# Two S4D convolution layers with routed FFNs: shorter setups, four-tile first transform step in layer two, new order

## The chip, the cores and the metric

The kernel runs on one core of a Trainium2 chip. A core has five engines with queues of their own: TensorE (PE, matmuls; PEld in the profile is its weight load), VectorE (DVE), ScalarE (ACT), GpSimd (POOL) and SyncE (SP, which issues most DMAs). The metric is the device time of one launch in microseconds. All data are 32-bit floating point numbers.

## The reference

`x` has 2048 tokens of 512 numbers. Each of two layers does

```python
x = x + S4D(layernorm(x))          # convolution over the tokens, per channel
x = x + routed_ffn(layernorm(x))   # SwiGLU FFN on two tokens, all others pass
```

The convolution's taps are built from the parameters (128 states for each channel), and it is done with transforms of twice the length:

```python
dt = exp(log_dt);  A = -exp(log_A_real) + 1j * A_imag
C = (C_real + 1j * C_imag) * dt[:, None]
P = exp((A * dt[:, None])[:, :, None] * arange(2048))
K = 2 * einsum("dn,dnl->dl", C, P).real
y = irfft(rfft(u, 4096) * rfft(K, 4096))[:2048] + u * D_skip
```

The routed part scores each token (`r = x @ w_r`), takes the two with the highest score, sends them through `(silu(x @ w_gate) * (x @ w_up)) @ w_down`, scales by `sigmoid(r)` and adds the result back. Both layers have the same parameters, so K is built once.

## The kernel before

The 512 channels are four chunks of 128; tokens lie as 128 partitions of 16 each (`z [128,16,128]`).

**Setups** (`setup`, lines L553 to L650). From A, C and dt they make planes of decays and phases for every (state, channel) pair: modulus and angle of C with Abs, a reciprocal, Arctan, Sin and corrections by quadrant (L592 to L618), fractions of turns in 32-bit integers (L620 to L631), shifted copies (L634), exponentials of the decay (L647). `setup(0, 1, ...)` does it for the first chunk, 128 wide, and keeps its planes in SBUF; `setup(1, 4, ...)` does it for the other three, 384 wide, and writes its planes to DRAM. An ACT function that is in another table than the one before needs an ACT_TABLE_LOAD.

**Kernel taps** (`KStep`, 32 of them, eight for each chunk). Each builds 1024 columns: POOL adds phases (L675) and multiplies decays (L689, L694), ACT makes sines and magnitudes (L705, L699, L708), DVE multiplies them (L716 to L723), PE sums over the states on 32-column tiles (pk, L731) and transforms (kq, L751).

**Convolution of a chunk** (`Conv`). A transform in two steps: the first, `f1a`, multiplies z with a block-diagonal constant into zf (recorded at L414, in `halves`, which writes a result with two 64-column tiles, weights of 128 rows). Each of its eight waves is four matmuls of 256 columns into a PSUM tile of one bank, 128x512, from a pair of such buffers (tag "f1"). `f1b` (L855) transposes it on DVE into g. Then, in eight groups, pu (second step, PE, L774), the product p with the kernel's spectrum (DVE, L864), the sums y (POOL and DVE, L877 and L879), pv (inverse step, PE), its copy v (ACT, L1108), a trip of v through DRAM (vd), and po (L919), the last inverse step, added to x. The last chunk of a layer takes another way to po (`fin_0`, `fin_t`, `fin_mm` L901).

**Routed part** (`Routed`). The choice of the tokens (about L1325 to L1470), pg and pu (up projections, PE, L1476) and pd (down, L1496), and the way back. `keep_awake` issues pairs of matmuls without use ("aw") where PE would have nothing to do.

**What sets the order.** Every unit of this work goes into an agenda with a number from the table `PLAN` (for each lane, one number for its k-th unit). `run` sorts the agenda by number and calls the units, and `in_order` binds the instructions of every engine to the order in which they are issued:

```python
def put_in(lane, f, *a):
    k = counts[lane] = counts.get(lane, -1) + 1
    agenda.append((PLAN[lane][k], (lane, k), f, a))
```

So an instruction that waits holds up all those behind it on its engine.

Of the kernel before, what the change touches and what calls it, by code (L numbers as in the profile page):

```python
# [19 lines left out]
D = 512  # L20
# [22 lines left out]
    ],  # L43
    x0=[103, 57, 141, 123],
    stat0=[105, 107, 104, 110, 99, 58, 59, 97, 161, 150, 144, 142, 128, 131, 124, 125],
    phase8=[
        94, 108, 109, 112, 85, 179, 199, 240, 259, 220, 346, 354, 364, 375, 358, 456, 470, 476, 492, 478, 606, 630, 631, 633, 589,
        707, 731, 782, 783, 791, 907, 933, 934, 946, 896, 1055, 1078, 1081, 1082, 1057,
    ],
    decay8=[  # L50
        87, 117, 121, 126, 106, 207, 247, 266, 277, 214, 371, 389, 390, 391, 393, 466, 474, 505, 509, 511, 601, 602, 603, 638,
        627, 740, 774, 775, 777, 727, 901, 929, 950, 960, 895, 1095, 1096, 1100, 1108, 1137,
    ],
    phase_0=[
        114, 113, 166, 152, 260, 264, 304, 330, 376, 407, 406, 445, 493, 538, 577, 518, 647, 676, 702, 690, 784, 787, 865, 815,
        947, 970, 1020, 1033, 1140, 1180, 1224, 1085,
    ],
    phase=[
        115, 146, 167, 165, 265, 270, 317, 339, 377, 408, 442, 446, 498, 544, 581, 539, 648, 677, 704, 692, 793, 798, 874, 886,
# [1813 lines left out]
```

## Time and profile before

| what | us |
|---|---|
| runs | 527.70, 527.08, 525.61 (median 527.08) |
| profiled execution, own time | 528.49 |
| its span | 526.7 |
| PE busy | 420.1 (80%) |
| DVE busy | 419.7 (80%) |
| ACT busy | 386.0 (73%) |
| POOL busy | 317.0 (60%) |

The span runs from the first to the last instruction of the profile; 1.8 us of the execution's own time lie outside it. Shares are averages over stages: first loads and setups (to about 65 us), kernel taps beside layer one's convolution (to about 330), layer one's routed part (to 390, overlapped with layer two's first chunk), layer two's convolution (to 475), and its routed part with the output. In lists by line, "x64" is a count of instructions, then come busy us and mean ns, then idle time ahead of them with what ended it. In lists in order of time the first number is the start and the second the duration of the row. A float matmul is two records.

### The profile page before, as it was taken

What the parts mean: (1) busy time and instruction counts of PE and PEld (TensorE: products, weight loads), DVE (VectorE), ACT (ScalarE), POOL (GpSimd) and SP (SyncE); (2) the same over time, 40 slices, a digit from 0 to 9 for tenths busy, and PEclk for the clock granted to TensorE, in tenths of its full rate; (3) what the DMA queues carried; (4) which work ended last, traced back from release to release, by engine and by line L of the source; (5) the groups of instructions that cost most, each with busy time, mean ns of one, the idle gap of its engine ahead of it and who ended that gap; (6) DMA issues with size and microseconds to landing.
All of it is one profiled execution on the core that took longest, in us unless ns stands there. A gap on an engine that the chain in (4) does not pass through costs nothing.

```text
span 526.7 us, 17177 instructions
## 1 busy us (share of the span) xinstructions
PE 420.1 (80%) x6976; PEld 322.5 (61%) x6976; DVE 419.7 (80%) x987; ACT 386.0 (73%) x862; POOL 317.0 (60%) x334
## 2 busy tenths in 40 slices
PE   1014377999989998799999986999799999878468
PEld 1013256888758976579857843557568788654134
DVE  7999997877958998688998479766667799889851
ACT  5998999999969978859755345643656958548892
POOL 0496689997958567736702945234606889977300
PEclk9999999999989999899999999799999999999779
DMA  7243988879655885667593999564574748846634
GB/s 254 85 195 113 297 326 326 231 188 233 181 147 169 221 222 174 222 181 214 134 324 125 400 361 338 213 277 145 180 242 140 244 142 276 270 168 287 240 155 167
DMA packets 67319, 115.96 MB, mean 220 GB/s; under 512 B 8708, under 2 KB 50984, under 8 KB 62504
## 3 DMA queue, kind: packets, MB, share of 16 engines
q1 hardware_dynamic: 67112, 114.85, 66.5%
q8 instruction: 55, 0.90, 0.7%
q14 instruction: 24, 0.20, 0.1%
q0 software_dynamic: 128, 0.02, 0.0%
HBM read 68.83 MB, written 39.72 MB: 206 GB/s over the span
## 4 chain that ended last, share of the span: by engine, by line
PE 23%; DMA 9%; DVE 8%; ACT 6%; POOL 3%; issue 1%; SPq 0%; DVEq 0%; ACTq 0%; POOLq 0%
DMA kfd<-kd 6%; PE zf L414 5%; PE pu L774 5%; PE pv L414 4%; PE po L919 2%; DMA v<-vd 2%; PE pd L1496 1%; PE po L414 1%; ACT xw L844 1%; DMA xs<-x 1%; ACT jw L943 1%; DVE g L855 1%; PE aw L414 1%; DVE stt L1158 1%; POOL y L879 1%
## 5 line engine op out<-in xcount | busy, mean ns | idle before, releaser
L879 POOL TENSOR_TENSOR y<-p 64x256 f32<-64x256 f32 x76 | 57.7, 759 | 71.5 <-DVE p L864 37.2
L723 DVE TENSOR_TENSOR sc<-tr,mg 128x1024 f32<-128x1024 f32 x64 | 77.2, 1212 | 2.1 <-POOL mg L694 1.7
L731 PE MATMUL pk<-sc 128*32 128x64 f32 x2048 | 39.2, 233 | 40.2 <-DVE sc L723 27.0
L731 PEld LDWEIGHTS pk<-sc 128*32 128x32 f32 x2048 | 33.5, 118 | 53.2 <-issue 32.0
L675 POOL TENSOR_TENSOR ph<-eight,far 128x768 int32<-128x768 int32 x32 | 53.0, 1663 | 18.0 <-ACT tr L708 17.6
L689 POOL TENSOR_TENSOR mg<-eight,far 128x768 f32<-128x768 f32 x32 | 53.6, 1675 | 9.2 <-DVE sc L718 6.7
L414 PE MATMUL zf<-z,d 128*64 128x256 f32 x384 | 53.4, 405 | 2.7 <-issue 2.1
L855 DVE STREAM_TRANSPOSE g<-zf 128x512 f32<-128x512 f32 x64 | 44.9, 708 | 10.1 <-PE zf L414 9.0
L751 PE MATMUL kq<-d1k,kt 128*64 128x128 f32 x512 | 38.5, 298 | 17.7 <-ACT rq0b L955 9.2
L414 PE MATMUL pv<-y,w 128*64 128x128 f32 x640 | 45.6, 279 | 8.6 <-POOL y L877 6.1
L1108 ACT ACTIVATE w<-pv 128x512 f32<-128x512 f32 x48 | 28.2, 589 | 27.6 <-PE pv L414 21.2
L414 PEld LDWEIGHTS pv<-y,w 128*64 128x64 f32 x640 | 37.8, 138 | 15.3 <-POOL y L877 9.7
L864 DVE TENSOR_TENSOR p<-pu,kf 128x1024 f32<-128x1024 f32 x32 | 39.0, 1219 | 9.5 <-PE pu L774 4.8
L751 PEld LDWEIGHTS kq<-d1k,kt 128*64 128x64 f32 x512 | 32.0, 150 | 23.5 <-ACT rq0b L955 9.4
L694 POOL TENSOR_TENSOR mg<-mg,f32s 128x512 f32<-128x512 f32 x32 | 34.3, 1072 | 16.1 <-ACT mg L683 12.6
L774 PE MATMUL pu<-g,w 128*64 128x128 f32 x640 | 42.6, 276 | 0.8 <-DVE g L855 0.8
L774 PEld LDWEIGHTS pu<-g,w 128*64 128x64 f32 x640 | 38.0, 135 | 5.7 <-issue 3.3
L877 POOL TENSOR_TENSOR y<-p 64x256 f32<-64x256 f32 x52 | 38.9, 750 | 3.1
L414 PE MATMUL pv<-p,w 128*64 128x128 f32 x384 | 38.7, 276 | 2.2 <-ACT w L1108 2.1
L414 PEld LDWEIGHTS zf<-z,d 128*64 128x64 f32 x384 | 27.8, 144 | 17.2 <-issue 3.5
L414 PE MATMUL pv<-p,w3b 128*64 128x128 f32 x384 | 38.1, 273 | 0.0
L708 ACT ACTIVATE tr<-ph,cst 128x1024 f32<-128x1024 f32 x32 | 35.6, 1114 | 0.4
(380 smaller groups left out, 1123.2 us busy)
## 6 DMA issues: line engine op xcount, KB each, us to landing
vd<-w SPq DMA_DIRECT2D x48, 256.0 KB, 2.7
v<-vd SPq DMA_DIRECT2D x24, 512.0 KB, 5.9
kf<-kfd SPq DMA_DIRECT2D x16, 512.0 KB, 6.9
wd<-in_wd SPq DMA_DIRECT2D x4, 2048.0 KB, 10.8
ks<-kd SPq DMA_DIRECT2D x48, 128.0 KB, 3.4
kfd<-kd SPq DMA_DIRECT2D x24, 256.0 KB, 3.9
x<-in_xr SPq DMA_DIRECT2D x4, 1024.0 KB, 5.8
z<-in_x SPq DMA_DIRECT2D x4, 1024.0 KB, 6.0
```

Source lines behind the costliest of these rows:

```text
L414: T.matmul(out[h : h + 64], w[:, h : h + 64], rhs, start=start, stop=stop, tile_position=(0, h))
L675: G.tensor_tensor(self.ph[:, :, 8:32].rearrange("p d (k i) -> p d k i", k=3), self.first(0).rearrange("p d (o i) -> p d o i", o=1).to_broa ...
L689: G.tensor_tensor(mg[:, :, 0:2, 8:32].rearrange("p d t (k i) -> p d t k i", k=3), self.first(1).rearrange("p (d t o) i -> p d t o i", t=2, ...
L708: A.activation(out, pa, AF.Sin, scale=-TURN, bias=halfpi)
L723: V.tensor_tensor(sc.rearrange("p d (t i) -> p d t i", t=3)[:, :, 0:3:2, :], t, self.mg[:, :, 0:3:2, :], op=OP.mult)
L731: T.matmul(self.pk[32 * g : 32 * g + 32, e, :], t[:, 0:32], t[:, 32:96], start=k == 1, stop=k == 0, tile_position=(0, 32 * g))
L751: T.matmul(self.pq[64 * ri : 64 * ri + 64, e].rearrange("p k g -> p (k g)"), self.kt[:, e].rearrange("p h b -> p (h b)"), d1k[:, 128 * ri ...
L774: T.matmul(pt[64 * par : 64 * par + 64, ri, q, :], w2[:, k1, 64 * ri : 64 * ri + 64], col(src, k1), start=True, stop=True, tile_position=( ...
L855: V.transpose(g[:, :, 16 * q : 16 * q + 16, :].rearrange("p k e t -> p e k t"), pf.rearrange("p (k t) e -> p e k t", t=2))
L864: V.tensor_tensor(pp, pu.rearrange("p (o r) q e -> p o r (q e)", o=1).to_broadcast([128, 2, 2, 2 * CH]), kf.rearrange("p r (o q) e -> p r ...
L877: E.tensor_tensor(y[64:128, :, par, :], p[1][ls, 0], p[0][ls, 1], op=OP.add)
L879: E.tensor_tensor(y[0:64, :, par, :], p[0][ls, 0], p[1][ls, 1], op=OP.subtract)
```

## The change

Three things are changed. First, the setup: a clamp goes into the maximum (`scalar_tensor_tensor` with two maxima), the quadrant corrections of the angle are three two-step operations that use two signs (ACT, Sign) instead of comparisons and multiplications, and the four products of u (by 64, -1, 31.5 and -0.5), their rounding, subtraction and scaling are each one operation 4n wide instead of separate ones of n and 2n. That is 13 DVE operations fewer for each of the two setups, and two ACT operations more. Second, the first transform step of layer two: `f1a_wide` makes four waves for each chunk, each four matmuls of 64 rows, 64 columns and 512 wide, one for each quarter of PE, into a PSUM tile of two banks (128x1024), of which there is one instead of two of one bank; `f1b_wide` transposes it in one DVE operation. Other users of the tag "f1" (the FFN's pg, pu and pd, `fin_0` of the last chunk, `keep_awake`) take halves of the same two-bank tile. Third, all numbers in `PLAN` are new.

The core of the diff; PLAN is shown with two lanes:

```diff
 PLAN = dict(
...
-    t_f1a=[
-        464, 478, 480, 489, 475, 493, 469, 473, 595, 614, 635, 604, 631, 618, 609, 620, 675, 737, 749, 751, 658, 694, 734, 713,
-    ],
+    t_f1a=[458, 462, 472, 440, 576, 611, 606, 594, 689, 710, 667, 684],
+    t_f1b=[463, 468, 473, 441, 579, 620, 607, 600, 695, 720, 668, 686],
...
-        cst = st([128, 4], "cst")
+        cst = st([128, 8], "cst")
+        for k, v in enumerate((64.0, -1.0, 31.5, -0.5)):
+            G.memset(cst[:, 4 + k : 5 + k], v)
...
-            S.append(lambda: V.tensor_tensor(mx, ar, ai, op=OP.max))
+            S.append(lambda: V.scalar_tensor_tensor(mx, ar, 1e-37, ai, op0=OP.max, op1=OP.max))
             S.append(lambda: V.tensor_tensor(sw, ar, ai, op=OP.min))
-            S.append(lambda: V.tensor_scalar(w, mx, 1e-37, None, op0=OP.max))
-            S.append(lambda: V.reciprocal(w, w))
+            S.append(lambda: V.reciprocal(w, mx))
             S.append(lambda: V.tensor_tensor(w, sw, w, op=OP.mult))
             S.append(lambda: A.activation(at, w, AF.Arctan))
-            S.append(lambda: V.tensor_tensor(w, ai, ar, op=OP.is_gt))
+            S.append(lambda: V.tensor_tensor(w, ar, ai, op=OP.subtract))
+            S.append(lambda: A.activation(w, w, AF.Sign))
+            S.append(lambda: A.activation(crt, crt, AF.Sign))
+            S.append(lambda: V.tensor_scalar(cit, cit, 0.0, -0.5, op0=OP.is_lt, op1=OP.add))
...
-            S.append(lambda: V.tensor_scalar(g1, at, 1.0 / (2 * math.pi), None, op0=OP.mult))
-            S.append(lambda: V.tensor_scalar(v1, g1, -2.0, 0.25, op0=OP.mult, op1=OP.add))
-            S.append(lambda: V.tensor_tensor(v1, v1, w, op=OP.mult))
-            S.append(lambda: V.tensor_tensor(g1, g1, v1, op=OP.add))
+            S.append(lambda: V.scalar_tensor_tensor(w, at, -math.pi / 4, w, op0=OP.add, op1=OP.mult))
+            S.append(lambda: V.scalar_tensor_tensor(w, w, -math.pi / 4, crt, op0=OP.add, op1=OP.mult))
+            S.append(lambda: V.scalar_tensor_tensor(ar, w, math.pi / 2, cit, op0=OP.add, op1=OP.mult))
             S.append(lambda: V.scalar_tensor_tensor(al, al, -1.0, dt, op0=OP.mult, op1=OP.mult))
-            S.append(lambda: V.tensor_scalar(v1, g1, -2.0, 0.5, op0=OP.mult, op1=OP.add))
-            S.append(lambda: V.tensor_scalar(w, crt, 0.0, None, op0=OP.is_lt))
-            S.append(lambda: V.tensor_tensor(v1, v1, w, op=OP.mult))
-            S.append(lambda: V.tensor_tensor(g1, g1, v1, op=OP.add))
-            S.append(lambda: V.tensor_scalar(v1, cit, 0.0, -0.5, op0=OP.is_lt, op1=OP.add))
-            S.append(lambda: V.tensor_tensor(g1, g1, v1, op=OP.mult))
...
-            S.append(lambda: V.tensor_scalar(pc[:, :, 0], u, 64.0, None, op0=OP.mult))
-            S.append(lambda: V.tensor_scalar(pc[:, :, 1], u, -1.0, None, op0=OP.mult))
-            S.append(lambda: V.tensor_copy(ip, pc))
-            S.append(lambda: V.tensor_tensor(pc, pc, ip, op=OP.subtract))
-            S.append(lambda: V.tensor_scalar(ip, pc, 2.0**31, None, op0=OP.mult))
-            S.append(lambda: V.tensor_scalar(bq[:, :, 0], u, 31.5, None, op0=OP.mult))
-            S.append(lambda: V.tensor_scalar(bq[:, :, 1], u, -0.5, None, op0=OP.mult))
-            S.append(lambda: V.tensor_copy(bi, bq))
-            S.append(lambda: V.tensor_tensor(bq, bq, bi, op=OP.subtract))
-            S.append(lambda: V.tensor_scalar(bi, bq, 2.0**31, None, op0=OP.mult))
+            S.append(lambda: V.tensor_tensor(q4.rearrange("p (k e t) -> p k e t", k=2, t=2), of4, by4, op=OP.mult))
+            S.append(lambda: V.tensor_copy(qi, q4))
+            S.append(lambda: V.tensor_tensor(q4, q4, qi, op=OP.subtract))
+            S.append(lambda: V.tensor_scalar(q4i, q4, 2.0**31, None, op0=OP.mult))
...
+        def f1a_wide(z, q, nm):
+
+            pf = ps.tile([128, 32, 32], F32, name=f"zf{nm}_{q}", tag="f1", bufs=1)
+            for s in range(2):
+                rows = slice(64 * s, 64 * s + 64)
+                for h in (0, 64):
+                    T.matmul(
+                        pf[h : h + 64, 16 * s : 16 * s + 16, :], d1[rows, 128 * s + h : 128 * s + h + 64],
+                        z[rows, :, 32 * q : 32 * q + 32], start=True, stop=True, tile_position=(64 * s, h))
+            return pf
+
+        def f1b_wide(g, q, pf):
+            V.transpose(g[:, :, 32 * q : 32 * q + 32, :].rearrange("p k e t -> p e k t"), pf.rearrange("p (k t) e -> p e k t", t=2))
...
-                self.y["f", q] = f1a(self.z, q, f"{self.layer}_{self.c}")
+                self.y["f", q] = (f1a_wide if self.layer else f1a)(self.z, q, f"{self.layer}_{self.c}")
...
-            t = ps.tile([128, 2, CH], F32, name=f"aw{i}", tag=("f1", "u")[i])
+            t = ps.tile([128, 2, CH], F32, name=f"aw{i}", tag=("f1", "u")[i], bufs=1 + i)
```

ACT, at the start of the program: the setups' functions and the table loads between them. Names with "su" are the setups' planes, in "su_bigB" and "su_w" the 384-wide ones; "dtb" is dt spread over partitions. Before:

```order
L599 ACT_TABLE_LOAD
L599 ACTIVATE su_113<-su_113 128x128
L602 ACT_TABLE_LOAD
L602 ACTIVATE su_113<-su_113 128x128
L603 ACTIVATE su_113<-su_113,cst 128x128
L647 ACT_TABLE_LOAD
L647 ACTIVATE su_113<-su_113 128x128
L601 ACTIVATE su_bigB<-su_w_108 128x384
L599 ACT_TABLE_LOAD
L599 ACTIVATE su_bigB<-su_bigB 128x384
L647 ACT_TABLE_LOAD
L647 ACTIVATE su_113<-su_113 128x128
```

and in the change:

```order
L598 ACT_TABLE_LOAD
L598 ACTIVATE su_117<-su_117 128x128
L600 ACTIVATE su_117<-su_117 128x128
L592 ACTIVATE su_bigB<-su_w_112 128x384
L593 ACTIVATE su_bigB<-su_w_112 128x384
L604 ACT_TABLE_LOAD
L604 ACTIVATE su_117<-su_117 128x128
L605 ACTIVATE su_117<-su_117,cst 128x128
L603 ACT_TABLE_LOAD
L603 ACTIVATE su_117<-su_117 128x128
L546 ACTIVATE dtb<-pdt 128x512
L603 ACTIVATE su_bigB<-su_w_112 128x384
```

The Sign (L600, behind Arctan at L598) is new, and Sin (L604) and Exp (L603) of the first setup now stand together ahead of the second setup's Arctan; of these twelve rows five are loads before, and three in the change. Up to the steady run of KSteps there are 13 before and 10 after.

PE, in layer two, where the first transform step of chunk 2 stands (zf_2; xw is its z) among the work of chunk 1 (pu_1, pv_1) and the output of layer one (po_0). Before:

```order
L414 MATMUL pv_1_4_5697<-y_1_4_5579,w_818 64x128 x8
L414 MATMUL zf_2_0_5714<-xw,d_64 64x256 x4
L414 MATMUL zf_2_3_5731<-xw,d_64 64x256 x4
L414 MATMUL zf_2_6_5740<-xw,d_64 64x256 x4
L414 MATMUL zf_2_1_5749<-xw,d_64 64x256 x4
L414 MATMUL pv_1_5_5756<-y_1_5_5686,w_818 64x128 x8
L414 MATMUL zf_2_5_5765<-xw,d_64 64x256 x4
L414 MATMUL zf_2_7_5771<-xw,d_64 64x256 x4
L414 MATMUL zf_2_4_5789<-xw,d_64 64x256 x4
L414 MATMUL zf_2_2_5797<-xw,d_64 64x256 x4
L414 MATMUL pv_1_6_5808<-y_1_6_5723,w_818 64x128 x8
```

and in the change:

```order
L412 MATMUL pv_1_2_5604<-y_1_2_5541,w_815 64x128 x8
L855 MATMUL zf_2_0_5616<-xw,d_64 64x512 x4
L766 MATMUL pu_1_6_5635<-g_1_5262,w_63 64x128 x8
L855 MATMUL zf_2_3_5654<-xw,d_64 64x512 x4
L412 MATMUL pv_1_4_5662<-y_1_4_5507,w_815 64x128 x8
L855 MATMUL zf_2_2_5686<-xw,d_64 64x512 x4
L412 MATMUL pv_1_5_5692<-y_1_5_5600,w_815 64x128 x8
L855 MATMUL zf_2_1_5704<-xw,d_64 64x512 x4
L412 MATMUL aw_5710<-d_64,sm 64x256 x2
L412 MATMUL pv_1_7_5716<-y_1_7_5684,w_815 64x128 x8
L766 MATMUL pu_2_0_5736<-g_2_5624,w_63 64x128 x8
```

Before, the eight waves (L414) stand nearly back to back, with one pv among them. Now the four waves (L855, 512 wide) have other matmuls between each of them and the next. In chunk 1 the four waves have only two aw and two small matmuls (pn) between them.

PE, near the end, around the choice of layer two's tokens (pi, pb, pr, pq, ph) and the first projection of its FFN (pg). Before:

```order
L414 MATMUL aw_6763<-d_64,sm 64x256 x2
L414 MATMUL aw_6779<-d_64,sm 64x256 x2
L414 MATMUL aw_6784<-d_64,sm 64x256 x2
L1414 MATMUL pi_6801<-b_14_6787,sm 8x1 x2
L1414 MATMUL pi_6801<-ones,sm 8x1
L1424 MATMUL pb_6812<-b_14_6787,ones 128x24
L1426 MATMUL pr_6813<-b_14_6787,sm 8x1 x2
L1443 MATMUL pq_6837<-b_23_6828,sm 8x32 x2
L1467 MATMUL ph_6857<-b_25_6843,b_26_6844 128x8
L1468 MATMUL ph_6857<-b_25_6843,b_19_6810 128x8
L1476 MATMUL pg_6862<-wgu,b_4_6679 32x448 x16
```

and in the change:

```order
L1424 MATMUL pi_6685<-b_14_6657,sm 8x1 x2
L1424 MATMUL pi_6685<-ones,sm 8x1
L1434 MATMUL pb_6698<-b_14_6657,ones 128x24
L1436 MATMUL pr_6699<-b_14_6657,sm 8x1 x2
L412 MATMUL aw_6715<-d_64,sm 64x256 x2
L1453 MATMUL pq_6718<-b_23_6710,sm 8x32 x2
L412 MATMUL aw_6723<-d_64,sm 64x256 x2
L412 MATMUL aw_6736<-d_64,sm 64x256 x2
L412 MATMUL aw_6739<-d_64,sm 64x256 x2
L1477 MATMUL ph_6742<-b_25_6727,b_26_6728 128x8
L1478 MATMUL ph_6742<-b_25_6727,b_19_6696 128x8
L1486 MATMUL pg_6747<-wgu,b_4_6581 32x448 x16
```

In the change four aw stand between pr and ph, where there was none.

More of the change, by code (lines that the diff above doesn't have):

```diff
@@ L181 @@
+    e_tt=[6, 20, 37, 22, 54, 59, 68, 82],
     e_y=[
[L182 to L191 removed]
@@ L573, in fplane @@
             def fplane(k):
-                return direct_plane(1, k) if direct else half(pair((10, 12, 6)[k % 3] if k else 0))
+                return direct_plane(1, k) if direct else half(pair((10, 12, 2)[k % 3] if k else 0))
             def iplane(k):
@@ L886, in i1_mm, with fin_0 @@
             return pv
-        def fin_0(c, q, layer, xc, tag):
-            po = (pso if tag == "po" else ps).tile([128, 16, 16], F32, name=f"po{layer}_{c}_{q}", tag=tag)
+        def fin_0(c, q, layer, xc, tag, po=None):
+            if po is None:
+                po = (pso if tag == "po" else ps).tile([128, 16, 16], F32, name=f"po{layer}_{c}_{q}", tag=tag)
             halves(po, ident, xc[:, :, 16 * q : 16 * q + 16], True, False)
@@ L1145, in fin_0 @@
             def fin_0(self, q):
-                self.y["o", q] = fin_0(self.c, q, self.layer, self.xc, ("f1", "po", "u", "misc")[q // 2])
+                if q < 2 and ("f1" not in self.y):
+                    self.y["f1"] = ps.tile([128, 2, 512], F32, name=f"po{self.layer}_{self.c}", tag="f1", bufs=1)
+                po = self.y["f1"][:, q, 0:256].rearrange("p (j e) -> p j e", j=16) if q < 2 else None
+                self.y["o", q] = fin_0(self.c, q, self.layer, self.xc, (None, "po", "u", "misc")[q // 2], po)
             def fin_t(self, q):
@@ L1260, in down_weights @@
             nc.sync.dma_start(t, wd[h])
-            wds[i] += [t[:DW, D * y : D * y + D] for y in range(8)]
+            wds[i].update({8 * h + y: t[:DW, D * y : D * y + D] for y in range(8)})
         cu[3].xload(new_xc(3))
@@ L1485, in ffn @@
                     A.preload_act_table(AF.Sqrt)
-                pu = [ps.tile([128, H], F32, name=f"pu{i}_0", tag="f1"), psum([128, H], "pu1_")]
+                pu = [two[:, 1, 0:H], psum([128, H], "pu1_")]
                 up(pu[0], 1, 0, H)
@@ L1509, in ffn @@
                         if h == 0:
-                            pd[d] = ps.tile([128, 256], F32, name=f"pd{i}_{d}", tag="f1")
+                            pd[d] = two[:, d, 256 * d : 256 * d + 256]
                         down(d, range(2 * h, 2 * h + 2))
@@ L1743, in build @@
             put_in("r1_n", lambda j=j: affine(cu[0].z, *cu[0].tabs, (j,), NORM0))
-        for k in range(8):
+        for k in range(4):
             put_in("r1_fa", lambda k=k: cu[0].f1a(k))
@@ L1751, in build @@
                     put_in("t_norm", C.norm, j)
-                for k in range(8):
+                for k in range(4):
                     put_in("t_f1a", C.f1a, k)
```

304 lines of the change are left out of this document (153 added, 151 removed), and 80 rows, old and new, of tables (decay, norm, out, prod_b).

## The prediction

> **What bounds the kernel now.** I read the share of each engine first, then a table by stages, then the groups and the order in time inside the stages that the change touches. The page gives no single bound:
>
> ```profile
> PE 420.1 (80%) x6976; PEld 322.5 (61%) x6976; DVE 419.7 (80%) x987; ACT 386.0 (73%) x862; POOL 317.0 (60%) x334
> PE 23%; DMA 9%; DVE 8%; ACT 6%; POOL 3%; issue 1%; SPq 0%; DVEq 0%; ACTq 0%; POOLq 0%
> ```
>
> PE and DVE tie at 80%, an average over stages. The second line, the chain that ended last, gives PE 23% of the span and nobody else over 9%; the rest of the chain is in short links. So the stages have to be read apart. The columns below are the stretch, its length, busy time of PE, its weight loads, DVE, ACT and POOL with counts, the granted PE clock, the DMA share and GB/s:
>
> ```profile
> 15.00:40.00 25.00, 1.94 (x64) 1.72 (x64) 24.55 (x53) 23.47 (x37) 18.30 (x16) 1.00 0.37 142
> 40.00:65.00 25.00, 9.76 (x224) 8.27 (x224) 24.01 (x47) 23.55 (x39) 16.88 (x16) 1.00 0.63 207
> 100.00:150.00 50.00, 44.70 (x1020) 39.08 (x1018) 39.04 (x57) 45.25 (x80) 42.28 (x39) 0.99 0.77 205
> 381.00:475.00 94.00, 87.62 (x1150) 69.45 (x1152) 75.52 (x138) 61.45 (x154) 65.74 (x82) 0.99 0.66 214
> 420.00:450.00 30.00, 29.64 (x422) 24.45 (x420) 27.29 (x41) 21.80 (x59) 26.09 (x34) 1.00 0.70 215
> 475.00:496.00 21.00, 12.82 (x98) 6.27 (x94) 18.67 (x81) 18.52 (x123) 13.14 (x12) 0.91 0.78 311
> 496.00:507.00 11.00, 6.02 (x36) 3.12 (x36) 8.98 (x40) 10.14 (x23) 0.92 (x1) 0.66 0.01 2
> ```
>
> The start (15 to 65) belongs to DVE and ACT together: 48.6 and 47.0 of 50 us, PE nearly unused. From 100 on PE, ACT and POOL are all above 84%. Layer two's stage of convolutions (381 to 475) is PE's: 87.6 of 94. In its middle, DVE (27.3 of 30) and POOL (26.1) follow close behind. The changed setups lie in the first stage, the new first transform step in the stage from 335 to 475.
>
> **The setups.** Rows of the 384-channel setup, with the 128-channel one for L610 and L625 (busy us, ns of one):
>
> ```profile
> L610 DVE TENSOR_TENSOR su_bigB<-su_bigB 128x384 f32<-128x384 f32 x1 | 0.9, 858 | 0.0
> L614 DVE TENSOR_SCALAR su_bigB<-su_w 128x384 f32<-128x384 f32 x1 | 0.3, 347 | 0.0
> L624 DVE CAST su_bigB<-su_bigB 128x768 int32<-128x768 f32 x1 | 0.8, 801 | 0.0
> L625 DVE TENSOR_TENSOR su_bigB<-su_bigB 128x768 f32<-128x768 f32 x1 | 0.9, 950 | 0.0
> L610 DVE TENSOR_TENSOR su<-su 128x128 f32<-128x128 f32 x1 | 0.3, 293 | 0.0
> L625 DVE TENSOR_TENSOR su<-su 128x256 f32<-128x256 f32 x1 | 0.4, 426 | 0.0
> ```
>
> Removed are eleven operations on n columns (L596, L608 to L618 without L612; 384 wide 0.35 to 0.86 each, sum 6.3) and ten of n or 2n (L622 to L631; sum 6.7). Added are one scalar and three two-step operations on n columns (0.35 + 3 x 0.55 = 2.0) and four on 4n = 1536. These last the trace does not show. From two at 768 (0.95 + 0.80) I take 1.75 for each of the two TENSOR_TENSOR, and about 0.97 each for cast and scaling, 5.4 in all; the bound above is twice the 768 row throughout (1.9, 1.6, 1.9, 1.8 = 7.2). So 13.0 - 7.4 = 5.6 of DVE time, 3.8 at the upper bound. The 128-channel setup gives 5.6 - 3.3 = 2.3. Together 7.8 us of busy time. Many of these short rows overlap their neighbours by up to 0.1, so from start to start it is 5.6 to 6.2.
>
> ACT is as full as DVE in that stage, so its bill decides how much of this arrives. The first 75 us hold 13 table loads, the commonest lines being
>
> ```profile
> L647 ACT ACT_TABLE_LOAD x4 | 5.1, 1283 | 0.1
> L705 ACT ACT_TABLE_LOAD x3 | 3.8, 1283 | 0.1
> ...
> 4.87 0.29 ACT L592 ACTIVATE su<-su 128x128 f32<-128x128 f32 x1
> 6.16 0.52 ACT L592 ACTIVATE su_bigB<-su_w 128x384 f32<-128x384 f32 x1 [1.00 <-DMA su_w<-in_cr]
> ```
>
> The order of the change holds three loads fewer up to the steady run of kernel-tap steps (13 to 10): 3 x 1.283 = 3.85. The four Sign operations are new; priced by the Abs rows they cost 2 x 0.29 + 2 x 0.52 = 1.6. ACT gains 2.2, DVE 5.6 to 6.2. Neither engine can run ahead of the other by much, since each KStep passes POOL, ACT, DVE and PE in turn, and both are full from 15 to 65. I take **-3.0**, nearer the smaller. The bounds are -2.2 and -6.2. POOL, 42.3 of 50 busy after 100, can eat part of it: that is a rival below.
>
> **The first transform step of layer two.** One wave now (chunk 1, order in time; last, the matmuls that follow):
>
> ```profile
> 381.23 7.66 PE L414 MATMUL zf<-z,d 128*64 128x256 f32 x64
> 388.72 1.92 PE L414 MATMUL po<-sm,lt 128*64 128x128 f32 x32
> 390.47 1.03 PE L919 MATMUL po<-v,d 128*64 128x512 f32 x4
> 391.33 0.86 PE L774 MATMUL pu<-g,w 128*64 128x128 f32 x12
> ...
> 382.36 0.72 DVE L855 STREAM_TRANSPOSE g<-zf 128x512 f32<-128x512 f32 x1 [0.56 <-PE zf L414]
> 388.32 1.33 DVE L855 STREAM_TRANSPOSE g<-zf 128x512 f32<-128x512 f32 x2
> ...
> L855 DVE STREAM_TRANSPOSE g<-zf 128x512 f32<-128x512 f32 x64 | 44.9, 708 | 10.1 <-PE zf L414 9.0
> L864 DVE TENSOR_TENSOR p<-pu,kf 128x1024 f32<-128x1024 f32 x32 | 39.0, 1219 | 9.5 <-PE pu L774 4.8
> L825 DVE TENSOR_TENSOR p<-pu,kd 128x512 f32<-128x512 f32 x3 | 2.1, 688 | 0.4 <-PE pu L414 0.3
> ```
>
> A matmul is two records. A wave of four (8 records) of 256 columns takes 0.86, as the row pair 390.47 to 391.33 does for two matmuls of 512 on two column tiles: two column tiles run together. A wide wave is four matmuls of 512 on four 64x64 tiles. If all four run together, that is one stream of 512, 0.86: what now takes two waves, 1.72, then takes 0.86. No row of before shows two row tiles at work. Bounds: 0.86 (all four together), 1.72 (the two rows one after the other). I take the lower, since the column tiles do it.
>
> Changing between tile shapes is shown: a 64-column matmul between 32-column ones,
>
> ```profile
> 155.89 1.10 PE L731 MATMUL pk<-sc 128*32 128x64 f32 x64
> 156.92 1.08 PE L919 MATMUL po<-v,d 128*64 128x512 f32 x4
> 158.02 1.10 PE L731 MATMUL pk<-sc 128*32 128x64 f32 x64
> ```
>
> takes 1.10 from start to start (156.92 to 158.02) where it takes 0.86 among its like: 0.24 for in and out. The Trainium skill, "TensorEngine Tiling (Array Packing)", Key Properties, says that changing the tiling mode, "not just tile", drains the TensorE. The row is for a change of column tiles, not of row tiles. By the rule the price falls due at the way in and out of each of 16 waves, 3.8 us, as the sum below has it; if a change of row tiles were free, the sum would be -10.5. A filled wave, one with other matmuls around it, costs 0.86 + 0.24 = 1.10 against 1.72: **-0.62**, and 16 of them would be -9.9.
>
> But the pair of one-bank buffers has become one of two banks, so a wave waits for the transpose of the wave before. From 128x512 to 128x1024 an elementwise row grows by 0.54 (0.688 to 1.219); the transpose should go from 0.708 to 1.25 (bounds 0.71 and 1.42). Where nothing is put between, a period is 1.10 + 0.22 + 1.25 + 0.06 = 2.6 (0.22 from the wave's last matmul to the transpose and 0.06 from there to the next matmul, estimates from such gaps in order of time), and a chunk 4 x 2.6 = 10.4 less the last tail, about 10.2. Chunk 1 takes 8.4 now (381.23 to 389.65, the end of its last transposes). Its four waves have two spare warm-up matmuls and some tiny ones between, so there the change **loses 1.8**. Chunk 0 shows
>
> ```profile
> 335.28 5.36 PE L414 MATMUL zf<-z,d 128*64 128x256 f32 x32
> 340.79 1.95 PE L414 MATMUL zf<-z,d 128*64 128x256 f32 x16
> 343.20 1.95 PE L414 MATMUL zf<-z,d 128*64 128x256 f32 x16
> 345.97 2.04 PE L774 MATMUL pu<-g,w 128*64 128x128 f32 x32 [0.82 <-DVE g L855]
> ```
>
> 10.6 from first zf to the last transpose, so +0.4 to +1.1: I take a gain of 0.5. In chunks 2 and 3 pv, pu and po stand between the waves: gains of about 1.5 (three of four filled, 1.9, less 0.4 of wait at the fourth) and 2.5 (all four). Sum: 0.5 - 1.8 + 1.5 + 2.5 = **-2.7**. The four or so further warm-up matmuls in this stretch (0.43 each) I count as nothing: 6.4 us of its 94 are idle on PE, and they cost 1.7 if that cover is gone. The transposes also free 16 x (2 x 0.708 - 1.25) = 2.7 of DVE's 75.5; DVE doesn't set the end there, so nothing is booked for it. Bounds: -9.9 if every wave is filled, about +1 if only chunk 3's are.
>
> **The tail.** From 475 to 496 ACT (18.5 of 21) and DVE (18.7) have the same work as before, so that length stays. The FFN that follows runs at a clock that had sunk to 0.66 in 496 to 507:
>
> ```profile
> 507.55 4.72 PE L1476 MATMUL pg<-wgu,b 128*32 128x448 f32 x32 [0.35 <-DVE b L1470]
> 347.94 3.21 PE L1476 MATMUL pg<-wgu,b 128*32 128x448 f32 x32
> ```
>
> The new order has 4 warm-up matmuls right before pg where there were none after pi. If they hold the clock, pg falls from 4.72 towards layer one's 3.21: up to -1.5. If not, 0. I take **-1.0**.
>
> **Sum.** -3.0 - 2.7 - 1.0 = -6.7 on this execution's own 528.49: 521.8. That execution lies 1.41 above the median of the runs (527.08), so the median is 520.4. New numbers for all other units move work without adding any; I cost this at nothing, because it reorders units around the same dependences, with a bound of +-3 in the range.
>
> **Rivals.**
>
> B, the single buffer turns into a queue on DVE. In 420 to 450 DVE is 27.3 of 30 busy, and a transpose that arrives just after a product L864 started waits 1.22. Then the next wave waits, and pu behind it on PE waits too. Of the 12 waves of chunks 1 to 3, eight meeting a product cost 8 x 1.22 = 9.8 us: 521.8 + 9.8 = 531.6, median about 530. It decides from about six waves on. For: both rows. Against: PE has other ready units between in chunks 2 and 3. Chance 0.15. The same page of the Trainium skill, under PSUM Bottleneck, states that tiling speeds up TensorE but not the evacuation of PSUM, which may become the bottleneck; nothing in before has the wide form to test it.
>
> C, the two row tiles run one after the other: a wave is 1.72 + 0.24, and 0.86 x 16 = 13.7 us are to be added: 535.5, median 534. For: no row shows row tiles together. Against: the column tiles do. Chance 0.07. That page states that tiles work independently, which speaks against C; no run here shows it.
>
> E, both savings arrive whole: DVE's 6.2 (ACT has slack from the three loads, POOL isn't the bound), waves filled nearly throughout (-9.9) and the tail's -1.5 give -17.6; with POOL's load (26.1 of 30) taking about two of it, -16: 512.5, median 511. For: PE and DVE are the busiest and both lose work. Against: ACT's 2.2 and chunk 1. Chance 0.18.
>
> D, the change of order takes back what the work saves, or POOL (42.3 of 50 us in 100 to 150) and the DMA queues hold the middle as they are: the start's gain is used up by 300 us and only the tail and half of chunk 3 remain, -1 - 1.2 = -2.2: 526.3, median 525. For: POOL's work is the same. Against: POOL starts earlier too. Chance 0.15.
>
> **How the numbers follow.** Forecast 0.45 (median 516 to 524), E 0.18, D 0.15, B 0.15, C 0.07. A measurement of this kernel tells about 0.5%, 2.6 us, from no change. Faster: the forecast, E and a little of D make 0.64; within 0.5%: most of D, the mild edge of B: 0.16; slower: B's rest and C: 0.20. The range leaves C and the far half of E out: 511 to 532; the forecast's own is 516 to 524.
>
> **What would show it.** The start: the eighth KStep's taps some 3 us earlier, with three loads fewer. Waves: in chunks 2 and 3 the start of one zf wave to the next matmul 1.10; 1.96 says C; 0.86 says that the drain isn't paid for this shape. L855's successor in the 128x1024 form at 1.25 us. Chunk 1 about 10.2 from first zf to the last transpose. B shows as idle time of PE before zf, released by DVE, over 5 us in all. Tail: pg under 4.2. I am wrong if the start gains 6 or nothing, or if the order outside these places moves more than 3 us.

## The result and the profile after

The changed kernel takes **512.60 us** (median of four runs, 511.63 to 515.37) against 527.39 (525.61 to 529.07) for the kernel before beside it: ratio **0.9728, 95% interval 0.9677 to 0.9780**, 14.8 us faster. Forecast were 520.4, with 511 to 532 as the range and 516 to 524 as the forecast's own. The direction is right and the time lies inside the wide range, but the gain is more than twice the 6.7 us of the sum; the time is that of rival E, and, as will be seen, for another reason than E's.

The page of the changed kernel (engine, busy time and share, count; then the chain that ended last):

```profile
PE 407.6 (79%) x6848; PEld 303.1 (59%) x6848; DVE 419.0 (82%) x945; ACT 380.3 (74%) x863; POOL 317.2 (62%) x338
PE 30%; DVE 24%; ACT 16%; DMA 11%; POOL 9%; issue 8%; SPq 1%; POOLq 0%; DVEq 0%; ACTq 0%
```

DVE's busy time is nearly what it was (419.7), though 42 operations are gone. Its transposes take 2.1 us less (44.9 before, 22.8 + 20.0 now) and the setups' rows 5.0 less, added up; other rows of the same count have grown instead (the sums y from 16.7 to 17.7, jn from 16.0 to 17.0). So the shares say nothing on where 13 us went. A cut of the span at two events that both kernels have does: the ninth KStep's taps on DVE (kt) and the last KStep's. First the kernel before, then the changed one, in the columns of the table by stages (stretch, length, PE, weight loads, DVE, ACT, POOL, granted clock, DMA share, GB/s):

```profile
0.00:98.90 98.90, 41.32 (x874) 33.41 (x876) 90.13 (x179) 87.68 (x148) 66.48 (x68) 1.00 0.67 230
98.90:277.80 178.90, 166.30 (x3494) 136.91 (x3490) 150.22 (x304) 148.47 (x254) 118.84 (x104) 0.98 0.71 202
277.80:526.70 248.90, 212.46 (x2614) 152.15 (x2612) 179.32 (x508) 149.85 (x461) 131.68 (x163) 0.95 0.64 229
```

```profile
0.00:99.40 99.40, 43.57 (x896) 35.05 (x898) 89.00 (x155) 86.38 (x151) 69.76 (x73) 1.00 0.66 222
99.40:264.60 165.20, 160.62 (x3466) 133.95 (x3464) 148.93 (x302) 144.55 (x252) 116.88 (x103) 1.00 0.78 219
264.60:513.50 248.90, 203.43 (x2494) 134.12 (x2489) 181.05 (x491) 149.41 (x461) 130.52 (x163) 0.95 0.65 231
```

To the ninth taps: 98.9 and 99.4. From there to the last taps: 178.9 and **165.2**. From there to the end of the span: 526.7 - 277.8 = 248.9 and 513.5 - 264.6 = 248.9, although PE has 9.0 us less work there (212.5 and 203.4). So the pair of profiles differs by +0.5, -13.7 and 0.0: all of the gain lies in a stage in which the change neither removes nor adds an instruction worth naming, only moves them. PE's idle time in it falls from 12.6 to 4.6 us. Part of the 13.7 may be the clock: it was granted at 0.98 there before and at 1.00 after, and the same PE work took 166.3 us in this profile and 162.3 to 162.5 in two others of the old order at 1.00 (e2, e4 below, 175.4 and 175.7 long). I call this stretch "the middle" below, the units up to the first agenda's end "the first half", and what comes behind (from layer one's last chunk on) "the second half"; the table of numbers is sorted once for each half.

### The profile page after: what moved, and what is told of

Read it like the earlier page. It is cut to its first block, busy times and chain, and to the rows that moved or that the text cites. A ratio compares the mean times of both kernels' runs of the same rounds, so it can differ in the third digit from the quotient of the medians.

```text
span 513.5 us, 16908 instructions
## 1 busy us (share of the span) xinstructions
PE 407.6 (79%) x6848; PEld 303.1 (59%) x6848; DVE 419.0 (82%) x945; ACT 380.3 (74%) x863; POOL 317.2 (62%) x338
## 4 chain that ended last, share of the span: by engine, by line
PE 30%; DVE 24%; ACT 16%; DMA 11%; POOL 9%; issue 8%; SPq 1%; POOLq 0%; DVEq 0%; ACTq 0%
PE pv L412 7%; POOL y L885 4%; POOL y L883 4%; DMA v<-vd 3%; PE zf L855 3%; ACT z L836 3%; PE pu L766 3%; PE po L926 2%; DVE g L861 2%; DMA vd<-w 2%; PE kq L743 2%; DVE sc L715 2%; PE pk L723 2%; ACT tr L697 2%; DVE p L870 2%
## 5 line engine op out<-in xcount | busy, mean ns | idle before, releaser
L412 PE MATMUL pv<-y,w 128*64 128x128 f32 x640 | 45.2, 280 | 7.0 <-POOL y L883 4.4
L743 PE MATMUL kq<-d1k,kt 128*64 128x128 f32 x512 | 37.7, 294 | 13.2 <-DVE kt L730 12.4
L412 PEld LDWEIGHTS pv<-y,w 128*64 128x64 f32 x640 | 36.4, 139 | 18.7 <-POOL y L883 10.1
L412 PE MATMUL zf<-z,d 128*64 128x256 f32 x256 | 36.2, 394 | 0.1
L691 ACT ACTIVATE ph<-ph 128x1024 f32<-128x1024 int32 x32 | 33.8, 1056 | 0.3
L510 POOL TENSOR_TENSOR eight<-eight,near 128x128 int32<-128x128 int32 (+5 forms) x36 | 28.2, 786 | 9.3 <-ACT eight L504 7.0
```

The costliest lines, as they stand in the source:

```text
L412: T.matmul(out[h : h + 64], w[:, h : h + 64], rhs, start=start, stop=stop, tile_position=(0, h))
L743: T.matmul(self.pq[64 * ri : 64 * ri + 64, e].rearrange("p k g -> p (k g)"), self.kt[:, e].rearrange("p h b -> p (h b)"), d1k[:, 128 * ri ...
```

## Experiments

Each kernel below has the kernel before or the changed kernel as its base. Times are medians; "middle" is the stage from the ninth to the last taps in its profile. Profiles with the same order of the first half scatter there: 178.9, 175.4, 175.7 and 178.8 for the old order (before, e2, e4, e6: mean 177.2), and 163.4, 161.1, 165.2, 161.9, 164.6, 165.0, 164.7 and 161.8 for the new (mean 163.5). The two groups don't touch.

### Which part of the change does it: e1 to e4

The diffs are the parts of the change themselves: for e1 the numbers of the first half's lanes (two of them here), for e2 the hunk of the setups, e3 both, e4 all that lies behind.

```diff
# e1, e3
-    x0=[103, 57, 141, 123],
+    x0=[68, 49, 144, 110],
# e2, e3
-            S.append(lambda: V.tensor_tensor(mx, ar, ai, op=OP.max))
+            S.append(lambda: V.scalar_tensor_tensor(mx, ar, 1e-37, ai, op0=OP.max, op1=OP.max))
...
# e4
+                self.y["f", q] = (f1a_wide if self.layer else f1a)(self.z, q, f"{self.layer}_{self.c}")
...
```

Where a plan has no place for an operation (old setups in the new order, new ones in the old), it stands beside the operations that it works with. The fences of edits in this section show parts of them; numbers of PLAN stand there in words.

> Only the numbers of the units of the first half (setups, kernel taps, layer one's first three chunks) are those of the change; setups, waves and the order of everything behind are as before. Theory 'order': the 10 us that the changed kernel has gained between 100 and 285 come from where units stand, so this kernel alone gains 6 to 11 us. Rival 'setups': the gain follows from fewer setup operations, so the order alone gains under 3 us. The prediction booked 0 within 3.

> Only the setups are the new ones, each new operation at the place of the old one that it replaces; order and waves as before. Theory 'order': 1 to 4 us faster, near the 3.0 that the prediction booked. Rival 'setups': 8 us or more faster, since the start is earlier and what follows moves with it.

> New setups and new order of the first half; layer two and everything from layer one's last chunk on as before. Both theories: 12 to 14 us faster, the whole gain, as the start of pg in layer one stands 14.4 earlier in the changed kernel. If the second half contributes by itself, under 11.

> Setups and first half as before; four-tile waves and the new order of the second half. If the second half gives nothing, within 1.5 us of before. By the prediction's terms (2.7 for the waves, 1.0 for the tail) 3.7 us faster.

Measured, beside 529.05 for the kernel before on the same chip:

| kernel | median us | ratio (95%) | ninth taps at | middle |
|---|---|---|---|---|
| e1, order of the first half alone | 523.40 | 0.9912 (0.9861 to 0.9963) | 109.0 | 163.4 |
| e2, setups alone | 529.27 | 1.0006 (0.9957 to 1.0056) | 102.3 | 175.4 |
| e3, both | 512.92 | 0.9693 (0.9586 to 0.9801) | 99.3 | 161.1 |
| e4, second half alone | 525.21 | 0.9929 (0.9879 to 0.9980) | 100.1 | 175.7 |

The stage rows of e1, e2 and e3, in this order, one fence each:

```profile
109.00:272.40 163.40, 161.02 (x3468) 133.97 (x3466) 149.19 (x304) 144.70 (x252) 116.79 (x103) 1.00 0.77 222
```

```profile
102.30:277.70 175.40, 162.26 (x3496) 134.59 (x3490) 150.03 (x303) 147.66 (x254) 118.70 (x104) 1.00 0.73 206
```

```profile
99.30:260.40 161.10, 159.00 (x3466) 133.49 (x3464) 149.05 (x304) 144.46 (x252) 116.98 (x103) 1.00 0.79 225
```

Three things follow. The middle's gain is the order's: e1 has it with the old setups (163.4), e2 doesn't with the new ones. The setups alone are worth nothing that these runs can tell (2.6 us either way); but with the new order they bring the ninth taps from 109.0 to 99.3, **9.7 us**. And the two don't add up: -5.6 and +0.2 apart, -16.1 together (between 10 and 22 by its interval). So none of the three fell where it was expected: e1 just short of its 6 to 11, e2 under its 1 to 4, e3 above its 12 to 14. The new order spends the first 100 us on other work; in e1, with the old setups, it pays 10 us of the middle's gain back there, and with the new setups nothing. e4 came out at -3.8 as the prediction's terms have it, but of its profile's 3.1 us below the one of before (span 523.6) 2.0 lie ahead of the last taps, where the two programs are the same; so that row doesn't carry the terms.

### Why the setups alone give nothing: e6

e2 had two wide operations ahead of the first KSteps, so I put them back to the old places (in words, e2 against e6):

```diff
-    setup2: u at 94.1, four products at 94.2
+    setup2: u at 111, four products at 132.1, one decay plane's Exp at 175.4
```

> The kernel before with the new setups alone, now with every new operation at the place of the old one (the run with setups alone had two wide operations ahead of the first KSteps); one decay plane is made later instead. If DVE's saving arrives in the old order: ninth taps 3 to 6 us earlier and the end 3 to 6 us earlier. If ACT holds it, by the two Sign operations and the same table loads: no gain, within 2 us.

531.54 against 527.35: ratio 1.0083 (1.0046 to 1.0121), 4.2 us longer, which neither branch of the expectation has, and the ninth taps at 104.4. Both kernels' ACT in order of time, first before, then e6:

```profile
12.79 0.31 ACT L599 ACTIVATE su<-su 128x128 f32<-128x128 f32 x1
13.12 1.28 ACT L602 ACT_TABLE_LOAD   x1
...
16.32 0.32 ACT L647 ACTIVATE su<-su 128x128 f32<-128x128 f32 x1
```

```profile
13.71 0.31 ACT L441 ACTIVATE su<-su 128x128 f32<-128x128 f32 x1
14.38 0.31 ACT L443 ACTIVATE su<-su 128x128 f32<-128x128 f32 x1 [0.36 <-DVE su L442]
14.60 0.29 ACT L444 ACTIVATE su<-su 128x128 f32<-128x128 f32 x1
14.91 1.28 ACT L447 ACT_TABLE_LOAD   x1
...
18.11 0.32 ACT L482 ACTIVATE su<-su 128x128 f32<-128x128 f32 x1
...
26.65 1.15 ACT L506 ACTIVATE ph<-eight 128x512 int16<-128x512 int16 x2 [1.95 <-POOL eight L353]
```

Between Arctan and the load for Sin two Signs now stand, and the first waits 0.36 for DVE's difference. The Exp behind is at 18.11 instead of 16.32. Half of these 1.8 us comes with the Signs; the other half stands ahead of the Arctan already (13.71 instead of 12.79), where ACT waits 2.77 instead of 1.75 for DVE. POOL's planes come later, and ACT waits 1.95 for them. The first taps stand 5.6 later (50.9 against 45.2), so these rows show a part of the delay and not all of it.

The table loads are no saving of the setups: in the first 75 us there are 13 before and in e2, 14 in e6 (the Exp that was moved adds one), and 10 in e1, which has the old setups in the new order, and in the changed kernel. The three that fell away are the order's. And the wide operations cost more than was booked. In the changed kernel:

```profile
L622 DVE TENSOR_TENSOR su_bigB<-su_bigB,su_w 128x1536 f32<-128x1536 f32 x1 | 2.4, 2362 | 0.0
L620 DVE TENSOR_TENSOR su_bigB<-su_w,cst 128x1536 f32<-128x1536 f32 x1 | 2.2, 2219 | 0.0
L621 DVE CAST su_w<-su_bigB 128x1536 int32<-128x1536 f32 x1 | 1.8, 1750 | 0.0
L623 DVE TENSOR_SCALAR su_bigB<-su_bigB 128x1536 int32<-128x1536 f32 x1 | 1.2, 1205 | 0.0
```

Added up, DVE's rows of both setups are 40.3 us before and 35.3 in the changed kernel: 5.0 less.

### What paces the middle in the old order: e5, e11 to e15

First I took the idle places of PE in the old order for the cause. What PE waited for in the middle of the kernel before (line that waited, what it waited for, us in total, times, longest), and in e3:

```profile
PE pk L731 <- issue: 2.3, 1, 2.3
PE zf L414 <- issue: 2.1, 1, 2.1
PE pv L414 <- ACT w L1108: 2.1, 3, 1.4
PE kq L751 <- DVE kt L738: 1.6, 3, 0.7
PE pk L731 <- ACT gk L761: 1.5, 2, 0.9
```

```profile
PE kx L255 <- issue: 0.6, 1, 0.6
PE kx L255 <- DVE xc L958: 0.5, 1, 0.5
```

These are single places, and the longest stand at the same instructions in the other profiles of that order (e2, e4, e6). e5 moves eight units of PE, six of them behind work that is ready and two forward (in words):

```diff
-    spectrum 13: 649   spectrum 14: 662   contract 15: 670   contract 10: 501   contract 25: 1073
+    spectrum 13: 653.1 spectrum 14: 666.1 contract 15: 674.5 contract 10: 504.1 contract 25: 1084.1
...
```

> The kernel before with seven units of PE moved behind the next one or two units of PE (spectrum of KSteps 13, 14 and 23; contract of 10, 15 and 25; one output product and one zf wave ahead of contract 15), and with them what hangs on them; nothing else changed. In the old order PE stands idle at just these places, 0.6 to 2.6 us at each and 6.5 together, in each of its three profiles. Theory 'PE's queue': the middle (ninth to last KStep) is paced by PE, so idle time taken away there comes off the end: 3 to 7 us faster. Rival 'the pace comes from POOL or ACT': the idle time moves to other places, within 1.5 us of before.

533.79 against 527.35, ratio 1.0113 (1.0051 to 1.0175): **6.4 us longer**, against both branches of the expectation. PE's waits in e5's middle:

```profile
PE pu L255 <- DVE p L666: 3.8, 4, 1.7
PE zf L255 <- issue: 2.0, 1, 2.0
PE pk L572 <- ACT gk L602: 1.9, 2, 1.2
PE kq L592 <- DVE kt L579: 1.6, 3, 0.7
PE pv L255 <- DVE p L666: 1.2, 1, 1.2
```

The 2.3 of pk are down to 1.0 (further down the same list), the 2.0 ahead of zf and the 1.6 of kq have stayed, and others have come: the middle is 180.2 long with 163.4 of PE work, so PE is idle for 16.8 us instead of 12.6. Mending single places of PE made it worse. That alone doesn't tell what paces the stage, since not all of them were mended. The next five kernels load one engine with work that changes nothing, for KSteps 8 to 31:

```diff
# e11, e12: spectrum
-                for e in range(4):
+                for e in [*range(4)] * (1 + (self.u >= 8)):
# e13, e14: turn
+                for _ in range(1 + (self.u >= 8)):
                     A.activation(gks[self.c][...], self.pq, AF.Copy)
# e15: back
+                    for _ in range(1 + (self.u >= 8)):
                         V.tensor_tensor(out, t, my, op=OP.mult)
```

> The kernel before with the spectrum matmuls of KSteps 8 to 31 issued twice, 24 times about 0.86 us of PE work more, 20.6 in all. If PE paces the old order's middle: the stage from ninth to last taps 18 to 21 us longer. If another engine's chain paces it and PE's 12.6 us of idle time are true slack: 8 to 12 longer.

> The kernel with new setups and the new order of the first half (second half as before), with the same 20.6 us of PE work more. PE is busy 159.0 of 161.1 us of this stage, so if it paces it there the stage is 19 to 21 us longer; under 15 if it doesn't.

> The kernel before with the ACT copy of each spectrum (gk, 0.59 us) issued twice for KSteps 8 to 31, 14.2 us of ACT work more. ACT is busy 148 of the stage's 176 to 179 us. If a chain through ACT paces the old order's middle: 9 to 14 us longer. If ACT only follows PE: under 5.

> The same 14.2 us on ACT in the kernel with new setups and new order of the first half. If PE alone paces it there: under 5 us longer than its 161; if ACT's place in the chain counts there too, as in the old order: 9 or more.

> The kernel before with one DVE product of each KStep from 8 on (0.69 us) issued twice, 16.6 us of DVE work more. If a chain through DVE paces the old order's middle: 10 to 17 us longer; else under 6.

Their middles, in the order e11 (old order), e12 (new), e13 (old), e14 (new), e15 (old):

```profile
102.70:286.00 183.30, 178.39 (x3846) 153.86 (x3842) 152.56 (x304) 148.77 (x254) 118.77 (x104) 1.00 0.69 198
```

```profile
98.90:274.80 175.90, 175.17 (x3818) 152.24 (x3816) 150.93 (x302) 145.70 (x252) 116.77 (x103) 1.00 0.72 206
```

```profile
103.00:284.10 181.10, 163.44 (x3492) 134.07 (x3488) 150.18 (x304) 159.78 (x276) 118.59 (x104) 1.00 0.70 199
```

```profile
99.30:269.20 169.90, 159.93 (x3466) 132.61 (x3464) 150.40 (x304) 156.56 (x274) 116.76 (x103) 1.00 0.75 213
```

```profile
99.90:281.30 181.40, 163.06 (x3500) 135.14 (x3496) 167.07 (x327) 148.14 (x254) 118.36 (x104) 1.00 0.69 199
```

| load | work added (busy) | old order, above 177.2 | new order, above 163.5 |
|---|---|---|---|
| PE | 16 (162.3 to 178.4; 159.0 to 175.2) | +6.1 | +12.4 |
| ACT | 11 to 12 | +3.9 | +6.4 |
| DVE | 17 | +4.2 | not run |

The medians of the whole kernels: e11 536.28 and e12 528.47 beside 530.46 for the kernel before (two, two and three runs), e13 532.65 (two runs), e14 521.34 (two) and e15 533.91 (eight) beside 527.12. (e13's profile is of the longer of its executions, 536.6 and 528.7, and e15's of its shortest; single profiles of one order differ by up to 4 us, so these sizes are rough.)

In the old order 11 to 17 us of work on any of the three cost 4 to 7, by the middles and by the medians: **none of the three paces it alone**, each has slack of its own. That the time goes in hand-overs from one queue to the next is what is left, and was not measured by itself; POOL, busy 119 of 178 us there, and the DMA queues were not loaded. In the new order PE's load comes through for three quarters or more (e12 against e3, which has the same program otherwise: 175.9 - 161.1 = 14.8 of 16.2), with PE busy 175.2 of 175.9. So there PE paces the stage, though not alone: ACT's load comes through for half (against the mean) to three quarters (8.8 against e3). The expectations of e11 and e12 were off in the size of the load (16 instead of 20.6); e11 cost less than its 8 to 12, e13 and e15 fell where their engine doesn't pace the stage, and e14 between its two branches.

### Which half of the new order: e9 and e10

Two mixtures, in which one group of lanes keeps its places relative to the KSteps' contract units and the other takes those of the other plan (in words).

```diff
# e9: setups and KSteps as in the change; e10: as before
-    front_mm, f1a, back_mm, ...: own plan
+    front_mm, f1a, back_mm, ...: the other plan, its places between one contract and the next
```

> First half with new setups; setups and all KStep units in the new order, the units of layer one's convolution in the old one (their old places between one contract and the next kept); second half as before. Measured: the stage from the ninth to the last KStep's taps, 178.9 us before and 161.1 with the whole new order. If the order among the KStep units carries the gain: under 167. If the convolution's places carry it: over 172.

> The kernel before with only the units of layer one's convolution in the new order (their new places between one contract and the next); setups, KStep units and second half as before. The same stage: if the convolution's places carry the gain, under 167; if the KStep units do, over 172.

565.6 and 577.7 us, against 530.5 for before. (In e9 the first columns of chunk 0 are normalized ahead of the end of the table of scales, so it computes other values there; the amount of work is the same.) Their middles:

```profile
106.70:315.60 208.90, 168.29 (x3512) 138.25 (x3508) 153.33 (x303) 148.05 (x254) 116.67 (x103) 0.98 0.61 174
```

```profile
110.80:327.70 216.90, 170.40 (x3442) 139.85 (x3440) 154.50 (x303) 145.99 (x251) 116.98 (x103) 0.94 0.57 164
```

By the letter both fall under "over 172", which for e9 names the convolution's places and for e10 the KSteps' units, so the two contradict each other: both are 30 to 38 us longer than the old order's 178.9 and 45 to 53 longer than the new one's mean. The mixtures can't say which half carries the gain. They show how much an order can cost: the same work takes from 161 to 217 us (the longest at a granted clock of 0.94, with 170 us of PE work for 159).

### The waves and the shared tile: e7, e8, e16 to e18

e7 puts the eight waves, the pair of one-bank buffers and the FFN's separate tiles back into the changed kernel; e8 is the changed kernel beside it.

```diff
-                self.y["f", q] = (f1a_wide if self.layer else f1a)(self.z, q, f"{self.layer}_{self.c}")
+                self.y["f", q] = f1a(self.z, q, f"{self.layer}_{self.c}")
...
```

> The changed kernel with the eight waves of 128 rows, pairs of one-bank buffers and the FFN's separate tiles back; setups and order as in the change. By the prediction's term for the waves (-2.7) it is 2 to 4 us slower than the changed kernel. If the waves' gain is eaten by the single buffer: within 1.5 us of the changed kernel.

> The changed kernel itself, for comparison on the same chip: 12 to 16 us faster than before.

517.67 against 513.77 (ratios to before 0.9827, 0.9769 to 0.9885, and 0.9777, 0.9725 to 0.9830): 3.9 us, as expected, in intervals that overlap. In the profiles the way from the last taps to the end is 514.5 - 262.3 = 252.2 with the old waves and 511.9 - 263.3 = 248.6 with the new, so it is the second half that differs. The clock isn't the same, though: granted on that way were 0.93 in e7 and 0.95 in e8, and e7's two shortest runs, 514.46 and 514.53, lie only 0.7 us above e8's median. So how much of the 3.9 is the waves' stays open. How a wave goes now, in chunk 1 and in chunk 2 (PE and one transpose, of the changed kernel):

```profile
370.18 1.20 PE L855 MATMUL zf<-z,d 64*64 64x512 f32 x8
...
372.76 1.09 PE L855 MATMUL zf<-z,d 64*64 64x512 f32 x8 [1.07 <-DVE b L1657]
373.78 1.08 PE L412 MATMUL aw<-d,sm 128*64 128x256 f32 x8
375.22 1.09 PE L855 MATMUL zf<-z,d 64*64 64x512 f32 x8 [0.36 <-DVE g L861]
...
403.67 1.09 PE L855 MATMUL zf<-xw,d 64*64 64x512 f32 x8 [0.31 <-DVE g L861]
404.69 1.09 PE L412 MATMUL pv<-y,w 128*64 128x128 f32 x16
406.13 1.09 PE L855 MATMUL zf<-xw,d 64*64 64x512 f32 x8 [0.35 <-DVE g L861]
...
404.82 1.25 DVE L861 STREAM_TRANSPOSE g<-zf 128x1024 f32<-128x1024 f32 x1 [0.16 <-PE zf L855]
```

Eight records of some 600 ns end within 1.09, and the next matmul starts at 1.02, where rival C had 1.96: all four tiles run together. So a wave costs 1.02 (403.67 to 404.69; 1.10 predicted), a transpose 1.25 (as predicted), the period is 2.46 (403.67 to 406.13; 2.6 predicted). The Trainium skill, "TensorEngine Tiling (Array Packing)", Key Properties, has tiles operate independently; these rows agree. In chunk 2 a wave still waits 0.31 to 0.35 for the transpose of the wave before, since the one unit between, 1.09, doesn't fill the 1.44 to its end. The Trainium skill, "Perfetto Trace Analysis", Matmuls, advises to rotate independent groups of matmuls through PSUM banks so that evacuation overlaps; here the single buffer's price is these 0.3 us a wave, far from rival B's 1.22, and PE's waits for a transpose ahead of a wave come to 1.4 us in all. (In chunk 1 two waves wait 1.07 and 1.06, for DVE's b and not for a transpose.)

The shared tile also has a price that I had not seen. The last FFN of the changed kernel:

```profile
493.58 4.76 PE L1486 MATMUL pg<-wgu,b 128*32 128x448 f32 x32 [0.33 <-DVE b L1480]
499.07 1.72 PE L1486 MATMUL pg<-wgu,b 128*32 128x224 f32 x32 [0.73 <-ACT b_w L1494]
```

The second row is pu, which writes the other bank of the same tile and waits for the Silu that reads pg. e16 and e18 give pg a tile of its own, e17 is the changed kernel beside e18.

```diff
-                pg = two[:, 0, 0:QW]
+                pg = psum([128, QW], "pg")
...
-                pu = [two[:, 1, 0:H], psum([128, H], "pu1_")]
+                pu = [two[:, 0, 0:H], psum([128, H], "pu1_")]
```

> The changed kernel with the FFN's pg in a tile of its own and pu in the two-bank tile, so that pu need not wait for the Silu that reads pg (0.73 us in the last FFN, 1.03 in the first). If that wait is on the way that sets the end: about 1 us faster than the changed kernel, 13 to 16 us under before; else the same as the changed kernel.

> The changed kernel again, beside the next run on the same chip: 12 to 16 us under before.

> The changed kernel with pg of the FFN in a tile of its own, again: 1 to 2 us under the changed kernel beside it, if the two waits of pu on the Silu (0.73 and 1.03 us) count; the same time, if what was seen before is the scatter of the runs.

The wait is gone in e18:

```profile
490.14 4.95 PE L1329 MATMUL pg<-wgu,b 128*32 128x448 f32 x32 [0.33 <-DVE b L1323]
494.93 3.20 PE L1329 MATMUL pu<-wgu,b 128*32 128x224 f32 x64
```

Times: e16 510.88 (ratio 0.9674, 0.9593 to 0.9754); e17 512.92 (0.9764, 0.9701 to 0.9828) and e18 512.18 (0.9741, 0.9682 to 0.9801) side by side. That is 0.7 us in the direction expected and not to be told from none.

## Why the prediction was wrong, point by point

The gain is the forecast's in its direction and rival E's in its size, and the size is luck: it comes from a term that stood in neither. **The step that failed** is the last of the sum: "New numbers for all other units move work without adding any; I cost this at nothing, because it reorders units around the same dependences, with a bound of +-3". The order took 13.7 us from the middle, by the pair of profiles and by the means of the groups (some 12 against the two profiles of the old order at a full clock), and it did so with the old setups too (e1). The row that should have given the bound stood in the prediction: in 100 to 150 PE was busy 44.70 of 50, and I wrote only that PE was "above 84%" from 100 on. In the next two stretches of 50 us it is busy 47.0 and 46.0 (and POOL, of which I said the same, 34.4 and 30.0). The three together have 12 us of idle time on the busiest engine, in a stage that the new table rearranges from end to end. An upper bound of 12 for the order, instead of 3, would have put 512 inside the forecast's own range. On the other side e9 and e10 show that no loss of 3 was a bound either. Both of the prediction's own signs of being wrong came: the start gained nothing, and the order moved more than 3. What the runs don't show is which of the moved units make the new order's waits shorter.

**Setups, -3.0.** Wrong in size and in kind. DVE saved 5.0 us of busy time and not 7.8: the four wide operations of the 384-channel setup took 7.5 us (rows above) where I had 5.4 and an upper bound of 7.2, and one of the two-step ones 1.46 for 0.55. The three table loads belong to the order (e1), not to the setups. In the old order the setups make the kernel 0.0 to 0.8% longer (e2, e6); in the new order they are worth 9.7 us at the ninth taps (e1 to e3, one profile of e1). That is more than DVE's 5.0 and than the -3.0 that I took; how much of it is the operations' work and how much the places that the old ones had to take in e1 isn't separated. In the changed kernel nothing of it can be seen at the ninth taps (99.4 against 98.9), because the order had spent it: my sign "the eighth KStep's taps some 3 us earlier" did not come (87.9 against 88.7). That the setups' gain and the order's place are one thing (-5.6 and +0.2 apart, -16.1 together) was no term of mine.

**Waves, -2.7.** The mechanism and the prices were right (1.02 for 1.10, 1.25, 2.46 for 2.6; chunk 1 took 370.18 to 380.10, 9.9 against 10.2 predicted), and in the change's own order e7 and e8 give 3.9, at unlike clocks. What the second half gives as a whole, with waves, tail and order, is less than the 3.7 booked for waves and tail: from the last taps to the end the thirteen profiles with the old second half have 246.7 to 252.8 (mean 249.8), the six with the new one 244.6 to 248.9 (mean 247.7). That is 2.1 us by the means, in groups that overlap, although PE has 9 us less work on that way. By times it is between nothing (e3 at 512.92 already has the whole gain) and e4's 3.8; the runs don't settle it.

**Tail, -1.0.** pg took 4.76 with the change and 4.72 before, so that pair shows nothing. Over all profiles, pg takes 3.2 to 5.2 with the second half in the new order (seven, mean 4.4) and 4.5 to 6.1 in the old (thirteen, mean 5.4): the sign and size fit, but both scatter by more than the term. The wait of 0.73 at pu, which I missed, takes most of it back.

**Rivals.** B did not come: PE's waits for a transpose are 0.3 each. C is refuted by the four tiles' rows. D is wrong in its main sentence: POOL did not hold the middle, which became 13.7 us shorter with POOL's work the same (118.8 and 116.9). E had the number, but by savings that arrive whole; what arrived was an order with less waiting, and PE and DVE do almost the work they did (in the middle 160.6 and 148.9 against 162.3 and 150.0 in e2).

## What to carry to other kernels

A new static order is a term of its own. Take the idle time of the busiest engine over the stages that it rearranges as the first bound of its gain (here 12.6 us, and the stage gained 12 to 14), and a much larger one for its loss. Work saved and its new order belong together, and neither need show alone. Where several in-order queues hand work round, idle places on one of them need not be the cause: load each engine by a known amount and see how much comes through, before mending anything. When tiles are merged, look at who else shares them: here a write to one half waited for a read of the other.

## What the runs showed of the hardware

Two of PE's gaps in the old order, 2.3 us inside one contract and 2.1 ahead of a zf wave, have nothing that released them ("issue"), and stand at the same instruction in several profiles of that order (2.1 to 2.6 and 1.5 to 2.4 us). In the kernel before the list of DMA packets has a transfer of 16 KB on the queue named "instruction" that begins at 144.9, 0.3 us ahead of the start of the first gap, and the one before it at 132.9; most others are 4 to 10 us apart. The second gap begins at 218.5, with such a transfer at 218.0; in e2 the two gaps begin at 148.5 and 219.6, with transfers at 148.2 and 219.7. That PE ran out of instructions there fits this, and was not tested. The same pg of 32 records took 4.76 and 3.21 in two profiles of the changed kernel (the second is e17's), and 4.50 to 6.07 in thirteen with the old second half. The clock that is granted there differs from run to run: 0.66 while pg took 4.76, 1.00 with 3.21, and 0.52 with e1's 6.07. And the kernel before scatters from 521.5 to 534.0 over all its runs, so a difference under 3 us needs rows of the profiles as well as times.
